# Decay attention with a squared-ReLU MLP: the weight loads issued from ScalarE's DMA queue

## The chip, the core and the metric

The kernel runs on one core of a Trainium2 chip. The core has five engines that run side by side, each with its own in-order stream of instructions: TensorE (PE in the profile; its weight loads are shown apart as PEld), VectorE (DVE), ScalarE (ACT), GpSimd (POOL) and SyncE (SP), which in this kernel does nothing but issue DMAs. They meet through semaphores. The metric is device time in microseconds; lower is better.

## The reference

Eight batches of eight heads, 576 positions, head size 64, so 64 heads (h counts them from 0) and 4608 tokens of width 512.

```python
scores = scale * q @ k.T                                # per head, 576 x 576
cum = cumsum(log(clip(f, 1e-4, 1)))
scores = where(causal, -1e9, scores + cum[:, None] - cum[None, :])
attn = exp(scores - max(scores)); attn /= attn.sum() + 1e-9
x = heads_side_by_side(attn @ v)                        # 4608 x 512
h = maximum(x @ w_in, 0)                                # w_in: 512 x 2048, float64
out = (h * h @ w_out).astype(float32)                   # w_out: 2048 x 512, float64
```

[...]

## The kernel before, in words

**Weights.** `weight_ops` is a generator that brings in 32 blocks of 128 rows by 512 doubles (512 KB each, `w0` to `w31`; even ones from `w_in`, odd ones from `w_out`) and turns each into a pair of 32-bit halves. Block by block it goes through: the load (line 172, `stage`), the magnitude on ScalarE (L181, `wmag`), a clamp and a shift on VectorE (L192, L197), two merges on VectorE (L202, L204, into `osb`), a rounding copy on ScalarE (L209) and a subtraction on GpSimd (L210). Two loads are issued at the start and then up to `DEPTH = 4` blocks ahead, at the point of the code that follows L204. Each block has a buffer of its own, so a load overwrites nothing that is in use.

**Attention.** A schedule written out by hand walks "slots", six to a head. For heads 0 to 13 one slot has a score matmul (L346, from the buffer `rl` that holds a head's q and k), a mask matmul (L348), an exponential on ScalarE (L362) and, two slots later, the product with v (L411, copied out by L425 and L426). The row maxima of the *next* head are found meanwhile: matmuls L313 from the buffer `rk`, a masked minimum on VectorE (L319, into `tcol`), and then five small DMAs per head (L325, `rl<-tcol`, 128 numbers each, 64 in the last) that lay the maxima as a row into that head's `rl`. They go from the last columns to the first: 448 to 575, 320 to 447, 192 to 319, 64 to 191, 0 to 63. The first score of a head takes columns 256 to 575, so it can start when the **first three** of its five rows have landed. Below, "the third row" is that third DMA.

**Around it.** Per head there is a load of `rk` (288 KB, L252, issued by GpSimd on a queue of its own), of `rl` (288 KB, L259), of v (160 KB, L266) and of two rows of decay (L246), and for every second head a normalisation: `cmp<-den` twice (L436), a reciprocal, `rdr<-cmp` (L441), `den<-rdr` twice (L444), then a product on GpSimd (L447). When the eight heads of a batch are done, VectorE splits the result (L464, L465) and the MLP starts (L477, L500), which from then on fills TensorE between the attention slots. From head 14 on another path with rounded halves is used; the weights are done by then.

**What sets the order.** At the end of the kernel `in_order` ties the instructions of TensorE, ScalarE, VectorE and GpSimd to the order in which the code wrote them. SP is not in that list: the order of its DMAs is the scheduler's, which works from its own estimate of when each can go. Every DMA that SP or ScalarE issues raises one of eight semaphores (DMAHW0 to DMAHW7), and before a semaphore is used again the issuing engine waits until the DMA that used it before has landed.

```python
LAG = 2                                   # slots from a score to its product with v
at((h - 1) * NU + int(x), int(2 * x) % 2, max_unit, h, i)   # maxima, a head ahead
in_order(tc, [getattr(mybir.EngineType, e) for e in ("PE", "Activation", "DVE", "Pool")])
```

Of the kernel before, what the change touches and what calls it, by code (L numbers as in the profile page):

```python
# [11 lines left out]
I32 = mybir.dt.int32  # L12
# [21 lines left out]
def decay_attention_relu2_kernel(  # L34
# [18 lines left out]
    nc = tc.nc  # L53
# [28 lines left out]
    def bank(use):  # L82
# [11 lines left out]
        out=mz[:, MW - P:], in_=mz[:, MW - P:], pattern=[[-1, P]],  # L94
# [6 lines left out]
        out=eye, in_=eye, pattern=[[-1, P]],  # L101
# [62 lines left out]
    def weight_ops():  # L164

        staged, mags = {}, {}

        def stage():
            i = len(staged)
            if i < NW:  # L170
                raw = staged[i] = wk.tile([P, 2 * DM], I32, name=f"w{i}", bufs=1)
                nc.sync.dma_start(out=raw, in_=(w_in, w_out)[i % 2][i // 2].bitcast(I32))

        def words(i):
            w = staged[i].rearrange("p (n t) -> p n t", t=2)
            return w[:, :, 0], w[:, :, 1]

        def magnitude(i):
            if i < NW:
                mags[i] = wk.tile([P, DM], F32, name="wmag", bufs=1)  # L180
                nc.scalar.activation(out=mags[i], in_=words(i)[1].bitcast(F32), func=AF.Abs)  # L181

        stage()
        stage()
        yield
        magnitude(0)
        yield
        for i in range(NW):
            low, high = words(i)
            mag = mags.pop(i)  # L190

            nc.vector.tensor_scalar(mag, mag, MAG_LOW, MAG_HIGH, ALU.max, ALU.min)  # L192
            yield
            w = wk.tile([P, DM], F32, name="osb")
            wi = w.bitcast(I32)

            nc.vector.tensor_scalar(  # L197
                wi, mag.bitcast(I32), 3, 0x3FFFFFFF, ALU.logical_shift_left, ALU.bitwise_and,
            )
            magnitude(i + 1)  # L200
            yield
            nc.vector.scalar_tensor_tensor(wi, high, -0x40000000, wi, ALU.bitwise_and, ALU.bitwise_or)  # L202
            yield
            nc.vector.scalar_tensor_tensor(wi, low, 29, wi, ALU.logical_shift_right, ALU.bitwise_or)  # L204
            while len(staged) < min(i + 1 + DEPTH, NW):
                stage()
            yield
            hl = wk.tile([P, 2, DM], F32R, name=f"w{i}", bufs=1)
            nc.scalar.copy(out=hl[:, 0], in_=w)  # L209
            nc.gpsimd.tensor_tensor(out=hl[:, 1], in0=w, in1=hl[:, 0].bitcast(F32), op=ALU.subtract)  # L210
            split_w.append(hl)
            yield
# [501 lines left out]
```

## Time and profile before

| | |
|---|---|
| device time, 3 runs | 1253.07 us median (1252.28 to 1254.52) |
| profiled execution | 1255.36 us, of which the span of the instructions is 1253.3 us |
| TensorE busy | 1193.5 us, 95% of the span |
| VectorE, ScalarE, GpSimd busy | 785.1, 702.0, 372.4 us |
| DMA | 71.90 MB, mean 57 GB/s |
| the 32 weight loads (L172) | issued between 1.4 and 165.5 us, all from SP |

A row of the timeline has the start, the duration, the engine, the line and what was done; in square brackets stands the engine's idle time just before it, and what ended that. Rows of SPq are the issuing of a DMA: how long the queue was occupied, not how long the data took. Rows with x2 or x3 give the stretch from the first to the end of the last. A row of `windows` has, for a stretch of the span, the busy time of each engine with its number of instructions in brackets, the granted clock, the share of time that the 16 DMA engines were busy, and GB/s.

### The profile page before, as it was taken

How to read it: one execution, taken by the hardware profiler on the slowest of the kernel's cores; microseconds unless marked ns; L12 is line 12 of the kernel's file. 1: busy time of each engine (PE TensorE's matmuls, PEld its weight loads, DVE VectorE, ACT ScalarE, POOL GpSimd, SP SyncE). 2: the span in 40 equal slices, each digit the busy share in tenths (PEclk: the TensorE clock that was granted, in tenths of full speed). 3: DMA queues.
4: the chain of work that ended last, by engine and by line, in shares of the span. 5: the costliest groups of instructions: out<-in, count | busy, mean ns of one | idle time of the engine just before them, and what ended most of it. 6: DMA issues, size and time to landing. Idle time of an engine off the chain costs nothing.

```text
span 1253.3 us, 23182 instructions
## 1 busy us (share of the span) xinstructions
PE 1193.5 (95%) x7652; PEld 1051.8 (84%) x7652; DVE 785.1 (63%) x2042; ACT 702.0 (56%) x1720; POOL 372.4 (30%) x512
## 2 busy tenths in 40 slices
PE   3877899999999999999999999999999999999998
PEld 2544687888989899999899989998998989999997
DVE  7658776666666767666656566667665766532332
ACT  3545455556666666665565556666666666632332
POOL 4323223333333333333322233334333333200000
PEclk9999999999999999999999999999999999999999
DMA  8857631112121112121201121211121212000000
GB/s 199 193 129 176 177 87 26 51 32 57 41 55 33 48 37 57 40 57 26 55 18 52 31 57 32 55 34 52 40 57 41 57 41 52 17 27 1 18 18 17
DMA packets 115639, 71.90 MB, mean 57 GB/s; under 512 B 97384, under 2 KB 97384, under 8 KB 115520
## 3 DMA queue, kind: packets, MB, share of 16 engines
q1 hardware_dynamic: 114400, 66.30, 21.7%
q0 software_dynamic: 1120, 4.13, 1.5%
q8 instruction: 61, 1.00, 0.3%
q14 instruction: 58, 0.48, 0.1%
HBM read 60.20 MB, written 9.88 MB: 56 GB/s over the span
## 4 chain that ended last, share of the span: by engine, by line
PE 63%; ACT 1%; issue 1%; POOL 1%; DMA 0%; DVE 0%; SPq 0%; POOLq 0%; DVEq 0%; ACTq 0%
PE bank L477 25%; PE bank L500 24%; PE bank L388 3%; PE bank L355 2%; PE bank L390 2%; PE bank L389 2%; PE bank L313 2%; PE bank L352 2%; DMA den<-rdr 0%; ACT ph L377 0%; ACT den L426 0%; ACT r L485 0%; ACT p L362 0%; POOL v L299 0%; ACT rl L281 0%
## 5 line engine op out<-in xcount | busy, mean ns | idle before, releaser
L500 PE MATMUL bank<-w,gh 128*128 128x512 f32 x1152 | 413.8, 400 | 0.0
L477 PE MATMUL bank<-xh,w 128*128 128x256 f32 x2304 | 330.7, 286 | 4.9 <-DVE tcol L319 4.9
L378 DVE TENSOR_TENSOR pl<-p,ph 128x320 fp32r<-128x320 f32 (+4 forms) x300 | 186.9, 623 | 206.6 <-ACT ph L377 197.1
L477 PEld LDWEIGHTS bank<-xh,w 128*128 128x128 f32 x2304 | 301.2, 190 | 13.8 <-DVE tcol L319 5.3
L500 PEld LDWEIGHTS bank<-w,gh 128*128 128x128 f32 x1152 | 217.6, 189 | 39.0
L485 ACT ACTIVATE r<-bank 128x256 f32<-128x256 f32 x288 | 110.4, 383 | 211.7 <-PE bank L477 198.3
L500 PE MATMUL bank<-w,gl 128*128 128x512 f32 x576 | 227.1, 394 | 0.2 <-DVE gl L488 0.2
L486 DVE TENSOR_TENSOR g<-r 128x256 f32<-128x256 f32 x288 | 127.3, 442 | 144.2 <-ACT r L485 143.4
L364 POOL TENSOR_SCALAR_AFFINE_SELECT p<-p 128x128 f32<-128x128 f32 (+1 forms) x250 | 81.5, 326 | 454.2 <-ACT p L362 313.5
L377 ACT CAST ph<-p 128x320 fp32r<-128x320 f32 (+4 forms) x300 | 124.4, 415 | 148.9 <-POOL p L364 147.1
L477 PE MATMUL bank<-xl,w 128*128 128x256 f32 x1152 | 185.3, 283 | 0.0
L319 DVE CUSTOM_DVE_ANT_0 bank<-bank,mz 128x256 f32<-128x256 f32 (+4 forms) x320 | 133.7, 432 | 45.9 <-PE bank L313 44.5
L477 PEld LDWEIGHTS bank<-xl,w 128*128 128x128 f32 x1152 | 158.9, 191 | 0.0
L362 ACT ACTIVATE p<-bank 128x320 f32<-128x320 f32 (+4 forms) x300 | 115.8, 386 | 71.7 <-PE bank L355 67.3
L488 DVE TENSOR_TENSOR gl<-g,gh 128x256 fp32r<-128x256 f32 x288 | 128.9, 448 | 35.7 <-ACT p L362 0.9
L313 PE MATMUL bank<-rk 66*128 66x320 f32 (+9 forms) x384 | 111.8, 318 | 24.8 <-DMA rk<-qkraw 13.4
L487 ACT ACTIVATE gh<-r 128x256 fp32r<-128x256 f32 x288 | 120.5, 418 | 9.1
L500 PEld LDWEIGHTS bank<-w,gl 128*128 128x128 f32 x576 | 109.3, 190 | 14.3 <-DVE gl L488 0.9
L313 PEld LDWEIGHTS bank<-rk 66*128 66x128 f32 (+3 forms) x384 | 68.7, 185 | 40.1 <-DVE tcol L319 17.1
L388 PE MATMUL bank<-pl,vh 128*65 128x320 f32 (+4 forms) x350 | 99.4, 284 | 1.6 <-ACT den L426 1.4
L389 PE MATMUL bank<-ph,v 128*64 128x320 f32 (+4 forms) x350 | 94.8, 271 | 0.0
L390 PE MATMUL bank<-ph,vh 128*65 128x320 f32 (+4 forms) x350 | 93.0, 271 | 0.0
(71 smaller groups left out, 1498.2 us busy)
## 6 DMA issues: line engine op xcount, KB each, us to landing
qkraw<-in_qk SPq DMA_DIRECT2D x50, 288.0 KB
v<-in_v SPq DMA_DIRECT2D x64, 160.0 KB
den<-rdr SPq DMA_DIRECT2D x64, 144.0 KB
out<-osb SPq DMA_DIRECT2D x36, 256.0 KB
w<-in_w_in SPq DMA_DIRECT2D x16, 512.0 KB
w<-in_w_out SPq DMA_DIRECT2D x16, 512.0 KB
rl<-in_qk SPq DMA_DIRECT2D x14, 288.0 KB
rk<-in_qk POOLq DMA_DIRECT2D x14, 288.0 KB, 4.7
```

What stands on the lines that cost most here:

```text
L313: nc.tensor.matmul(ps[:m, :n], st["r2"][:rows, q0:q0 + m], st["kl0"][:rows, k0:k0 + n], start=True, stop=True,)
L319: nc.vector.tensor_tensor_reduce(out=ps[:m, :n], in0=ps[:m, :n], in1=mz[:m, mo:mo + n], op0=ALU.add, op1=ALU.min, scale=-1.0, scalar=init, ...
L377: nc.scalar.copy(out=ph[:kn, :n], in_=p[:kn, :n])
L378: nc.vector.tensor_tensor(out=pl[:kn, :n], in0=p[:kn, :n], in1=ph[:kn, :n].bitcast(F32), op=ALU.subtract,)
L388: nc.tensor.matmul(acc[:D + 1, o], vh, pl[:kn, i], start=first, stop=False)
L389: nc.tensor.matmul(acc[:D, o], vl, ph[:kn, i], start=False, stop=False)
L390: nc.tensor.matmul(acc[:D + 1, o], vh, ph[:kn, i], start=False, stop=last)
L477: nc.tensor.matmul(ph[:, :T], w[:, s, cc], x[:, cc, :], start=(cc == 0 and k == 0), stop=(cc == NCC - 1 and k == 2),)
L486: nc.vector.tensor_tensor(out=g, in0=r, in1=r, op=ALU.mult)
L487: nc.scalar.activation(out=gh, in_=r, func=AF.Square)
L488: nc.vector.tensor_tensor(out=gl, in0=g, in1=gh.bitcast(F32), op=ALU.subtract)
L500: nc.tensor.matmul(po, g[:, ts], w[:, s], start=(fc == 0 and k == 0), stop=(fc == NF - 1 and k == 2),)
```

## The change

The one call that issues a weight load is made on ScalarE in place of SP. ScalarE's stream gets 32 DMA instructions, SP's loses them.

```diff
         def stage():
             i = len(staged)
             if i < NW:
                 raw = staged[i] = wk.tile([P, 2 * DM], I32, name=f"w{i}", bufs=1)
-                nc.sync.dma_start(out=raw, in_=(w_in, w_out)[i % 2][i // 2].bitcast(I32))
+                nc.scalar.dma_start(out=raw, in_=(w_in, w_out)[i % 2][i // 2].bitcast(I32))
```

ScalarE is in the list of `in_order`, so a load now stands where the code wrote it. The streams of TensorE, VectorE and GpSimd are the same as before; ScalarE's computing instructions keep their order; SP's is rearranged in its first 150 DMAs.

**SP at the start.** Numbers such as 138 tell buffers apart: `w_100`, `w_102`, `w_136`, `w_138`, `w_140`, `w_168` are blocks 0 to 5. SP before, from the decay's store to the last maxima of head 0:

```order
L152 DMA cum_dr<-qkraw 64x576
L259 DMA rl<-in_qk 64x1152
L246 DMA rk_77<-cum_dr 2x576
L246 DMA rl<-cum_dr 2x576
L172 DMA w_138<-in_w_out 128x1024
L172 DMA w_140<-in_w_in 128x1024
L325 DMA rl<-tcol 1x128x1 x3
L172 DMA w_168<-in_w_out 128x1024
L325 DMA rl<-tcol 1x128x1
L266 DMA v<-in_v 128x5x64
L325 DMA rl<-tcol 1x64x1
```

SP now, at the same place:

```order
L259 DMA rl<-in_qk 64x1152
L246 DMA rl<-cum_dr 2x576
L237 DMA qkraw<-in_qk 64x1152
L325 DMA rl<-tcol 1x128x1 x3
L246 DMA rk_76<-cum_dr 2x576
L325 DMA rl<-tcol 1x128x1
L325 DMA rl<-tcol 1x64x1
```

The weight loads are gone from around the three rows that head 0's first score needs; a load of `qkraw` (288 KB, for head 14) that stood far later is now ahead of them, and three loads of v, which are not in this piece, have moved to the very start.

**ScalarE at the start.** ScalarE now, with the semaphores that each instruction waits for (the engine's name for a computing engine, DMAHW for a landed DMA):

```order
L181 ACTIVATE wmag<-w_100 128x512 [waits DMAHW0_49]
L181 ACTIVATE wmag<-w_102 128x512 [waits DMAHW3_49,DVE_49]
L172 DMA w_136<-in_w_in 128x1024 [waits DMAHW2_49]
L172 DMA w_138<-in_w_out 128x1024 [waits DMAHW5_49]
L172 DMA w_140<-in_w_in 128x1024 [waits DMAHW7_49]
L209 CAST w_142<-osb 128x512 [waits DVE_49,Activation_49]
L181 ACTIVATE wmag<-w_136 128x512 [waits DMAHW2_49,DVE_49]
L172 DMA w_168<-in_w_out 128x1024 [waits DMAHW5_49]
L209 CAST w_174<-osb 128x512 [waits DVE_49,Activation_49]
```

Blocks 2, 3 and 4 stand behind the second magnitude, which waits for VectorE, and each waits for a DMA that has to land first.

**ScalarE and SP between heads 5 and 6.** `w_628` and `w_682` are blocks 13 and 14. ScalarE now; before, the rows are the same without the two DMAs:

```order
L362 ACTIVATE ph_612<-bank3_609 128x192
L172 DMA w13_628<-in_w_out 128x1024
L362 ACTIVATE pl_633<-bank1_630 64x64
L209 CAST w9_638<-osb_600 128x512
L362 ACTIVATE ph_644<-bank2_641 128x448
L362 ACTIVATE pl_655<-bank3_652 128x256
L181 ACTIVATE wmag_660<-w11_485 128x512
L362 ACTIVATE ph_666<-bank1_664 128x320
L425 COPY xt0_289<-bank0_614 64x320
L426 COPY den_669<-bank0_614 1x320
L172 DMA w14_682<-in_w_in 128x1024
L362 ACTIVATE pl_687<-bank2_684 128x320
```

SP before, from the end of head 5's maxima to those of head 6:

```order
L325 DMA rl<-tcol 1x64x1
L172 DMA w_628<-in_w_out 128x1024
L246 DMA rk_77<-cum_dr 2x576
L441 DMA rdr<-cmp 128x9
L259 DMA rl<-in_qk 64x1152
L246 DMA rl<-cum_dr 2x576
L325 DMA rl<-tcol 1x128x1
L172 DMA w_682<-in_w_in 128x1024
L444 DMA den<-rdr 64x576 x2
L325 DMA rl<-tcol 1x128x1 x3
```

SP now has the same rows there without the two weight loads. Head 3 is where more than that differs. SP before:

```order
L325 DMA rl<-tcol 1x128x1
L436 DMA cmp<-den 64x1x9 x2
L325 DMA rl<-tcol 1x128x1 x3
L172 DMA w_428<-in_w_in 128x1024
L266 DMA v<-in_v 128x5x64
L325 DMA rl<-tcol 1x64x1
```

SP now, at head 3:

```order
L325 DMA rl<-tcol 1x128x1
L436 DMA cmp<-den 64x1x9
L325 DMA rl<-tcol 1x128x1
L266 DMA v<-in_v 128x5x64
L436 DMA cmp<-den 64x1x9
L325 DMA rl<-tcol 1x128x1 x2
L325 DMA rl<-tcol 1x64x1
```

A load of v has moved ahead of head 3's third row; block 10 (`w_428`), which was issued behind that row, is now issued by ScalarE.

## The prediction

> **What bounds the kernel now.** After the busy line of the page (TensorE at 95%) I read the windows that cut the span where its character changes, then TensorE's timeline in the stretch with idle time.
>
> ```profile
> 0.00:13.40 13.40, 0.00 (x0) 0.00 (x0) 9.36 (x12) 5.29 (x7) 7.67 (x21) 1.00 0.80 206
> 13.40:134.20 120.80, 86.79 (x375) 58.41 (x376) 83.56 (x224) 60.14 (x138) 38.13 (x46) 0.97 0.75 176
> 134.20:200.00 65.80, 64.25 (x369) 53.52 (x370) 48.35 (x109) 33.59 (x80) 17.60 (x17) 0.98 0.35 97
> 200.00:1253.30 1053.30, 1042.44 (x6910) 939.83 (x6908) 643.88 (x1698) 603.03 (x1497) 309.00 (x430) 1.00 0.16 39
> ```
>
> TensorE sets the time. After 134.2 us it is busy for 64.25 of 65.80 and 1042.44 of 1053.30 us: nothing that happens to loads there can move the end much. Its idle time is in front: 13.40 us before the first matmul and 120.80 - 86.79 = 34.0 us up to the MLP's first matmul. All but seven of the 32 loads fall before that point (the 25th is the row at 130.09 further down), so what the change is worth is decided there, and a microsecond won there is one at the end. Where TensorE waits:
>
> ```profile
> 23.00 0.87 PE L346 MATMUL bank<-rl 128*128 128x320 f32 x1 [5.30 <-DMA w<-in_w_out]
> 50.13 0.51 PE L346 MATMUL bank<-rl 128*128 128x320 f32 x1 [2.19 <-DMA rl<-tcol]
> 60.17 0.54 PE L346 MATMUL bank<-rl 128*128 128x320 f32 x1 [2.37 <-DMA rl<-tcol]
> 69.91 0.51 PE L346 MATMUL bank<-rl 128*128 128x320 f32 x1 [1.77 <-issue]
> 82.59 0.76 PE L346 MATMUL bank<-rl 128*128 128x320 f32 x1 [4.68 <-DMA rl<-tcol]
> 93.45 0.51 PE L346 MATMUL bank<-rl 128*128 128x320 f32 x1 [1.56 <-DMA rl<-tcol]
> 104.33 0.51 PE L346 MATMUL bank<-rl 128*128 128x320 f32 x1 [2.63 <-DMA rl<-cum_dr]
> ...
> 126.70 1.75 POOL L447 TENSOR_TENSOR xt<-xt,den 128x576 f32<-128x576 f32 x1 [0.74 <-DMA den<-rdr]
> 128.49 1.75 DVE L464 CAST xh<-xt 128x1024 fp32r<-128x1024 f32 x1 [1.29 <-POOL xt L447]
> 134.20 2.08 PE L477 MATMUL bank<-xh,w 128*128 128x256 f32 x8 [4.93 <-DVE tcol L319]
> ```
>
> The seven L346 rows are the first scores of heads 0, 3, 4, 5, 6, 7 and 8. Their waits sum to 20.5 us. The releaser's name varies, but I take all seven for the third row of maxima: that is the DMA issued last among what the score reads. The eighth wait, 4.93 us, is the MLP's start; VectorE was late there because `den` landed late, 1.29 us of its time.
>
> **Why the third row is late.** A small DMA that nothing stands before, and one with bulk around it:
>
> ```profile
> 43.08 2.13 SPq L436 DMA_DIRECT2D cmp<-den  x2
> 45.17 0.85 POOL L252 DMA_DIRECT2D rk<-in_qk  x1 [3.96 <-PE bank L313]
> 46.40 1.17 SPq L325 DMA_DIRECT2D rl<-tcol  x2
> 46.54 0.96 DVE L438 TENSOR_SCALAR cmp<-cmp 128x9 f32<-128x9 f32 x1 [0.63 <-DMA cmp<-den]
> 47.62 0.60 SPq L172 DMA_DIRECT2D w<-in_w_in  x1
> ```
>
> The `cmp` pair is issued by 45.21 and VectorE goes on at 46.54: 1.33 us after the end of the issue. Head 3's third row is the first of the two at 46.40, issued by about 46.98, yet its score starts at 50.13: 3.15 us, with no weight load near, but with GpSimd's 288 KB on another queue, issued at 45.17. So two things hold the third row: loads in flight on *any* queue, and loads ahead on SP's own. The rows where weights stand ahead:
>
> ```profile
> 15.98 0.36 SPq L172 DMA_DIRECT2D w<-in_w_out  x1
> 16.39 0.43 SPq L172 DMA_DIRECT2D w<-in_w_in  x1
> 16.92 1.81 SPq L325 DMA_DIRECT2D rl<-tcol  x3
> ...
> 68.35 0.59 SPq L172 DMA_DIRECT2D w<-in_w_out  x1
> 69.36 0.34 SPq L441 DMA_DIRECT2D rdr<-cmp  x1
> 73.52 0.59 SPq L172 DMA_DIRECT2D w<-in_w_in  x1
> 74.20 2.09 SPq L444 DMA_DIRECT2D den<-rdr  x2
> 76.38 2.11 SPq L325 DMA_DIRECT2D rl<-tcol  x3
> 98.67 0.58 SPq L172 DMA_DIRECT2D w<-in_w_out  x1
> 99.30 1.15 SPq L325 DMA_DIRECT2D rl<-tcol  x2
> ```
>
> Head 0: two loads ahead, third row issued by 18.73, score at 23.00, 4.27 us. Less the quiet 1.33 that is 2.9 us for two loads, 1.5 us each, my price of a load that is in the way.
>
> **When the loads go now.** A load stands behind a ScalarE instruction; the ends of these in the trace of before tell when it can go:
>
> ```profile
> 10.72 0.67 ACT L181 ACTIVATE wmag<-w 128x512 f32<-128x512 f32 x1 [1.42 <-DVE osb L197]
> 65.02 0.33 ACT L362 ACTIVATE ph<-bank 128x192 f32<-128x192 f32 x1
> 71.70 0.42 ACT L426 COPY den<-bank 1x320 f32<-1x320 f32 x1
> 96.74 0.36 ACT L426 COPY den<-bank 1x256 f32<-1x256 f32 x1
> ```
>
> Blocks 3 and 4 go from 11.4 us instead of 15.98, block 13 at 65.4 instead of 68.35, block 14 at 72.1 instead of 73.52, block 17 at 97.1 instead of 98.67. So the loads come 1.4 to 4.6 us sooner (block 2, formerly among the first, later). Those that stood ahead of a third row clear earlier; those that stood behind one move into its window, beside GpSimd's load.
>
> **The terms**, gains as plus, ends in brackets.
> - Head 0: +2.0 (0 to 2.9). Two loads leave SP's queue and are early, but `qkraw`'s 288 KB is new there, and by the order the third row waits on the semaphore that block 4 raises; so not the whole price.
> - Head 3: -1.5 (-0.6 to -2.1). A load of v now stands ahead of its third row, at least an issue (0.60, as at 47.62), at most that and one load's 1.5. Block 10 comes earlier too. I take the upper half.
> - Heads 5 and 7: -1.0 and -0.5 (0 to -1.5 each). Block 13, and by the same order block 16, moves from behind the last row to the time of the third; one load's price is the end.
> - Head 6: +1.5 (0 to 4.7, its whole wait). Block 13 no longer precedes `rdr`, nor block 14 `den`, for which SP waits with the three rows behind it; one load's price.
> - Head 8: +2.0 (0.6 to 2.6). Block 17 was between its rows: 0.58 us of issue, and one load's 1.5; its wait is the cap.
> - Head 4: 0; no load of weights between its rows before or now. Its wait stays, by GpSimd's load.
> - MLP's start: +1.0 (0 to 1.3). The chain that ends in `den` passes block 20 here:
>
> ```profile
> 115.65 0.35 SPq L172 DMA_DIRECT2D w<-in_w_in  x1
> 116.09 1.07 SPq L441 DMA_DIRECT2D rdr<-cmp  x1
> 122.52 1.13 SPq L444 DMA_DIRECT2D den<-rdr  x2
> 130.09 0.34 SPq L172 DMA_DIRECT2D w<-in_w_in  x1
> ...
> L172 SPq DMA_DIRECT2D w<-in_w_out x16: 343/500/627, 2.1 to 165.5; - x16
> ...
> PEld bank L411 <- ACT pl L362: 2.2, 4, 1.0
> ...
> DVE xt L138 <- DMA xt<-in_f: 0.6, 1, 0.6
> ```
>
> `rdr` to `den` took 6.4 us there. The gain cannot pass VectorE's 1.29 us of waiting; after that its own work is next.
> - ScalarE: -0.5 (0 to -11.2). On SP an issue took 0.34 to 0.63 us; I take the same, 0.45, on ScalarE, for the trace has none there. 25 loads before 134.2 us make 11.2 us. ScalarE is busy 60.14 of 120.80 us, and TensorE's largest wait for it at the products with v is 2.2 us in all. In seven heads a late exponential only shortens the wait for the third row, which does not depend on ScalarE. That cover is why the term is small; without it each load costs its 0.45. The seven loads after 134.2 lie beside 64.25 us of TensorE work: 0, or 3.2 if that cover went.
> - The start: -0.3 (0 to -1.5). `in_f`, which was alone, now goes beside block 0; VectorE already waits 0.6 us for it, and a load's price is the end. The v loads at the head of SP's queue go while it has nothing else to issue: 0.
>
> The sum is 2.0 - 1.5 - 1.5 + 1.5 + 2.0 + 1.0 - 0.5 - 0.3 = +2.7 us. The profiled execution took 1255.36 us, of which the span is 1253.3; that would become 1252.7. The median of the runs, 1253.07, lies 2.3 us under that execution, and less 2.7 it is **1250.4 us**.
>
> **The rivals.**
> - *The gates stay.* Being on another queue and somewhat earlier does nothing; only SP's time for issuing is saved: 0.36 + 0.43, 0.59 + 0.59 and 0.58, 2.6 us ahead of third rows, against 0.6, 1.5, 0.5 and 0.3 of losses above. That is -0.3: 1253.4. For it speaks head 3, held with a load on another queue alone; against it, that the loads' times do shift. [...]
> - *ScalarE becomes the gate* (slower). Its stream is in order, so a load that waits for its semaphore, or whose issue is long, stops the exponential behind it, then the product with v two slots later. Fully exposed it is 11.2 us against gains of 3.2: 1261; half exposed, 1255.5. I put it at 1258. It decides from about 0.2 us a load on TensorE's path ((2.7 + 2.5) / 25). Against it: the cover above, and that by the order loads mostly wait for DMAs that were issued long before.
> - *The gates open.* Heads 0, 6, 8 and the MLP's start gain their upper ends, 11.5 us, and heads 5 and 7 lose nothing: less 0.6, 0.5 and 0.3 it is 10.1, so 1243.0. Against it: VectorE finishes the maxima not much earlier than SP issues them, and GpSimd's load stays.
>
> That the change does not do what it says is excluded by the order.
>
> **How the numbers follow.** A measurement of this kernel tells about 0.2%, 2.5 us, from no change. Forecast, 0.36, of which 0.29 is over that bound and 0.07 within; the gates stay, 0.27, within; ScalarE, 0.22, slower; the gates open, 0.15, faster. Faster 0.44, same 0.34, slower 0.22. The forecast's own range is 1247 to 1252.5. The range of 8 in 10 reaches down to the open gates and up to most of ScalarE's case: 1243 to 1257.
>
> **What would show it.** The waits before L346 at heads 0, 6 and 8 shrink, those at heads 3 and 5 grow, that of head 4 stays; L464 waits less for L447; ScalarE's idle time before L362 shrinks by about 0.45 us a load while the product's wait for it hardly grows. I am wrong if the sum of the seven waits stays near 20 us, if waits of L411 for L362 reach 5 us, or if anything after 200 us changes by over 1 us.

## The result: slower by 0.6%, and the profile after

The changed kernel took **1262.77 us** (median of 7 runs, 1259.53 to 1264.3) against 1254.52 us for the kernel before (7 runs, 1251.19 to 1259.52) beside it: a ratio of **1.0057, 95% interval 1.0033 to 1.0081**. Timed once more later, 1261.65 against 1254.93 us, 1.0056 (1.0037 to 1.0076). The ratios with intervals, here and below, are estimated from the runs of both kernels; they are not quotients of two medians, which would be 1.0066 here. The prediction, 1250.4 us and faster, was wrong, and its range ended at 1257.

The profiled execution of the changed kernel took 1259.53 us, the quickest of the seven, with a span of 1257.8 us. First the windows, cut at this kernel's own first matmul (17.51 us) and its MLP's start (140.11 us); columns as before.

```profile
0.00:17.51 17.51, 0.00 (x1) 0.03 (x1) 7.23 (x12) 4.67 (x6) 7.17 (x20) 1.00 0.93 220
17.51:140.11 122.60, 87.11 (x375) 58.72 (x375) 85.08 (x224) 60.65 (x139) 39.13 (x46) 0.95 0.71 167
140.11:206.00 65.89, 65.03 (x368) 53.88 (x369) 48.36 (x109) 33.55 (x80) 17.15 (x17) 0.96 0.34 92
206.00:1257.80 1051.80, 1040.70 (x6911) 938.71 (x6909) 641.85 (x1698) 603.10 (x1497) 307.23 (x430) 1.00 0.16 39
```

From the MLP's start on it took 65.89 + 1051.80 = 1117.7 us, against 1119.1 before; in all profiles here it is between 1115.8 and 1119.1. So, as the prediction held, the loss is decided in front. What it missed is the first row: the first matmul is 4.1 us later, 17.51 against 13.40. The stretch from there to the MLP took 122.60 instead of 120.80.

A profile is a single execution, and this stretch varies from one to the next. A second profile of the same kernel, of a run of 1263.01 us, has this row for it:

```profile
17.32:144.59 127.27, 91.37 (x376) 61.75 (x376) 87.40 (x224) 60.90 (x139) 39.05 (x46) 0.91 0.67 161
```

The MLP's start is 4.5 us later there, and nearly all of that is TensorE's busy time, 91.37 instead of 87.11 us, at a lower granted clock, 0.91 instead of 0.95. So a wait or a start read from one profile says where time goes, and only the medians say which kernel is slower. TensorE's waits in the first profile, from its timeline:

```profile
17.51 0.82 PE L313 MATMUL bank<-rk 128*128 128x256 f32 x2 [17.51 <-DMA rk<-qkraw]
29.37 1.41 PE L346 MATMUL bank<-rl 128*128 128x320 f32 x2 [6.74 <-DMA rl<-tcol]
46.80 0.78 PE L346 MATMUL bank<-rl 128*128 128x320 f32 x2 [1.83 <-issue]
58.07 0.78 PE L346 MATMUL bank<-rl 128*128 128x320 f32 x2 [3.06 <-DMA rl<-tcol]
67.67 0.78 PE L346 MATMUL bank<-rl 128*128 128x320 f32 x2 [1.94 <-issue]
78.09 0.78 PE L346 MATMUL bank<-rl 128*128 128x320 f32 x2 [2.48 <-DMA rl<-tcol]
88.62 0.78 PE L346 MATMUL bank<-rl 128*128 128x320 f32 x2 [2.53 <-DMA rl<-tcol]
99.72 0.81 PE L346 MATMUL bank<-rl 128*128 128x320 f32 x2 [3.46 <-DMA rl<-tcol]
110.05 0.78 PE L346 MATMUL bank<-rl 128*128 128x320 f32 x2 [0.46 <-DMA rl<-tcol]
...
140.11 2.07 PE L477 MATMUL bank<-xh,w 128*128 128x256 f32 x8 [3.92 <-DVE tcol L319]
```

The rows are heads 0, 2, 3, 4, 5, 6, 7 and 8. Head 2, at 46.80, did not wait before. Against the starts shown before, head 3 is late by 7.9 us (58.07 - 50.13), head 6 by 6.0, head 8 by 5.7 and the MLP by 5.9. So all of the loss arises by head 3, and heads 6 and 8 give back 2 us of it. SP's timeline, at the start and at heads 2 and 3:

```profile
1.46 0.57 SPq L259 DMA_DIRECT2D rl<-in_qk  x1
2.08 2.52 SPq L266 DMA_DIRECT2D v<-in_v  x3
9.87 1.33 SPq L244 DMA_DIRECT2D rk<-qkraw  x2
...
20.26 0.51 SPq L237 DMA_DIRECT2D qkraw<-in_qk  x1
20.82 1.94 SPq L325 DMA_DIRECT2D rl<-tcol  x3
...
40.08 0.48 SPq L325 DMA_DIRECT2D rl<-tcol  x1
40.67 0.62 SPq L266 DMA_DIRECT2D v<-in_v  x1
41.38 3.22 SPq L325 DMA_DIRECT2D rl<-tcol  x4
...
50.77 0.55 SPq L325 DMA_DIRECT2D rl<-tcol  x1
51.42 0.61 SPq L266 DMA_DIRECT2D v<-in_v  x1
52.13 0.59 SPq L436 DMA_DIRECT2D cmp<-den  x1
52.84 2.17 SPq L325 DMA_DIRECT2D rl<-tcol  x3
```

`rk<-qkraw` (the first matmul's last input) was issued at 9.87 and let it go at 17.51. Three loads of v stand ahead of it. Head 0's third row, third of the group at 20.82, has the load of `qkraw` ahead. At heads 2 and 3 a load of v (for heads 3 and 4) has slipped in ahead of the third row. None of these is a weight load: they are SP's other DMAs, which the scheduler put in a new order once the weight loads had left. Counted from the start they are the fourth and the fifth load of v. Before the change the fourth stood between the fourth and the fifth row of head 3, and the fifth in the same place at head 4: the first five loads of v have all moved ahead.

### The profile page after: what moved, and what is told of

The parts are those of the page before. It is cut to its first block, busy times and chain, and to the rows that moved or that the text cites. A ratio compares the mean times of both kernels' runs of the same rounds, so it can differ in the third digit from the quotient of the medians.

```text
span 1257.8 us, 23157 instructions
## 1 busy us (share of the span) xinstructions
PE 1192.8 (95%) x7652; PEld 1051.3 (84%) x7652; DVE 782.5 (62%) x2042; ACT 702.0 (56%) x1720; POOL 370.7 (29%) x512
## 4 chain that ended last, share of the span: by engine, by line
PE 76%; ACT 3%; issue 1%; DVE 1%; POOL 1%; DMA 1%; SPq 0%; DVEq 0%; POOLq 0%; ACTq 0%
PE bank L477 30%; PE bank L500 28%; PE bank L388 4%; PE bank L313 3%; PE bank L355 3%; PE bank L390 3%; PE bank L389 3%; PE bank L352 3%; DMA den<-rdr 0%; ACT r L485 0%; ACT p L362 0%; ACT den L426 0%; ACT ph L377 0%; ACT gh L487 0%; ACT rl L281 0%
```

## The experiments

The median of the kernel before was 1255.31 us in the first group of four runs, 1254.65 in the second, 1255.12 in the third and 1254.93 in the fourth; each ratio is against the kernel before on the same chip. Most kernels below fix SP's order: a function ties SP's first 158 DMAs (190 where weights are on SP) one behind another, as `in_order` does for the other engines. Only the list differs. The tie by itself, on the scheduler's own new order, was not run.

```diff
-    in_order(tc, [getattr(mybir.EngineType, e) for e in ("PE", "Activation", "DVE", "Pool")])
+    sp_in_order(tc, SP_ORDER); in_order(tc, [getattr(mybir.EngineType, e) for e in ("PE", "Activation", "DVE", "Pool")])
```

**1. The order or the queue.** The changed kernel, with SP's DMAs in the order of before, less the weight loads:

```diff
 weight loads: nc.scalar.dma_start      # as changed
-SP_ORDER: the scheduler's
+SP_ORDER: as before the change, without L172
```

> The changed kernel with SP's DMAs tied to the order that they had before the change (the 32 weight loads stay on ScalarE). Theory O (the rearranged order on SP is what costs): the first matmul starts at 13.4 to 15 us instead of 17.5, head 0's first score before 25 us, the MLP's first matmul at or before 134 us, and the ratio to before is 0.996 to 1.001. Theory Q (the second queue is what costs: weight loads from ScalarE run beside SP's small DMAs at the start, whatever SP's order): first matmul still at 16.5 us or later and a ratio of 1.004 to 1.008.

Measured: 1255.29 us, ratio **0.9992 (0.9977 to 1.0008)**. The queue by itself is worth nothing that shows, by the interval between -2.9 and +1.0 us; the rearranged order carries the loss. TensorE's waits in this kernel:

```profile
12.61 0.82 PE L313 MATMUL bank<-rk 128*128 128x256 f32 x2 [12.61 <-DMA rk<-qkraw]
24.59 1.41 PE L346 MATMUL bank<-rl 128*128 128x320 f32 x2 [6.71 <-DMA rl<-tcol]
52.50 0.78 PE L346 MATMUL bank<-rl 128*128 128x320 f32 x2 [2.25 <-issue]
62.21 0.81 PE L346 MATMUL bank<-rl 128*128 128x320 f32 x2 [2.04 <-DMA rl<-tcol]
72.52 0.78 PE L346 MATMUL bank<-rl 128*128 128x320 f32 x2 [2.35 <-DMA rl<-tcol]
82.61 0.78 PE L346 MATMUL bank<-rl 128*128 128x320 f32 x2 [2.08 <-issue]
93.80 0.78 PE L346 MATMUL bank<-rl 128*128 128x320 f32 x2 [3.56 <-DMA v<-in_v]
103.64 0.78 PE L346 MATMUL bank<-rl 128*128 128x320 f32 x2 [0.20 <-issue]
...
134.55 2.08 PE L477 MATMUL bank<-xh,w 128*128 128x256 f32 x8 [6.01 <-DVE tcol L319]
```

Heads 6 and 8 wait 2.08 and 0.20 instead of 4.68 and 2.63, 5.0 us less, as the prediction said in kind. Against that, head 0 waits 1.4 more, head 7 2.0 more and the MLP's start 1.1 more; head 2 does not wait. The MLP starts 0.35 us later than before. The gains are there and are given back.

Head 0's longer wait begins on SP, at the copy of the decay (L246) that stands ahead of the rows:

```profile
13.14 0.60 SPq L259 DMA_DIRECT2D rl<-in_qk  x1
18.57 0.32 SPq L246 DMA_DIRECT2D rk<-cum_dr  x1
19.33 2.46 SPq L325 DMA_DIRECT2D rl<-tcol  x4
```

SP waited 4.8 us there for the decay's store (`cum_dr<-qkraw`, issued at 10.49 and 12.50) to land; before the change it waited 1.2 us, and the rows went from 16.92 and not from 19.33. ScalarE issues blocks 2 to 4 between 10.73 and 12.33 us in this kernel, while before blocks 3 and 4 went at 15.98 and 16.39, behind that wait. From 10 to 20 us the DMA engines moved 266 GB/s here and 183 before. So the weight loads now run beside the store; that they are what makes it late fits these numbers and was not tested by itself. The wait is 4.5 to 5.5 us in the five profiles with the weights on ScalarE and the old order at the start.

**2. The two loads moved at the start, one at a time,** each in the kernel of experiment 1:

```diff
 L259 rl<-in_qk
+L266 v<-in_v  x3        # a_v_early, and b_v_early with the weights on SP
 L244 rk<-qkraw x2
 ...
 L246 rl<-cum_dr
+L237 qkraw<-in_qk       # a_q_early
 L325 rl<-tcol x3
```

> As the kernel with SP's old order, but the three loads of v that the change moved to the very start (heads 0, 1, 2) stand there again; everything else on SP as before. Theory O, with the v loads as the cause of the late first matmul: first matmul at 16.5 to 17.5 us, and 3 to 4 us more time than with the old order. Theory Q: no different from the old order within 1 us.

> As the kernel with SP's old order, but the load of qkraw for head 14 stands ahead of head 0's rows of maxima, as the change has it. Theory O, with qkraw as the cause of head 0's longer wait: first matmul as with the old order, the wait before head 0's first score 1 to 3 us longer than with the old order, and that much more time. Theory Q, or block 5 as the cause of that wait: no difference over 0.5 us at head 0.

> The kernel before (all weight loads on SP) with only the three v loads moved to the start, behind the load of rl, as the change has them. Theory O: first matmul 2 to 4 us later than 13.4, ratio 1.002 to 1.004, without any load on ScalarE. Theory Q: 13.4 to 14, ratio 1.000.

Measured: with the v loads early 1255.52 us, 1.0002 (0.9989 to 1.0014); with `qkraw` early 1255.76 us, 1.0006 (0.9990 to 1.0021); in the kernel before, the v loads early cost 1256.74 us, 1.0020 (1.0003 to 1.0037). With the v loads early the first matmul started at 17.29 and not at 12.61, but head 0's wait fell from 6.71 to 4.21 us, and the MLP started 0.8 us later. With `qkraw` early head 0 waited 7.97 us, and the MLP again started 0.8 us later. Theory O had the late first matmul right, and on ScalarE's queue its cost wrong: 3 to 4 us were expected of the v loads. Neither alone is the loss.

**3. The start and the rest, halved.** `c_start` has the new order up to head 0's first row and the old one behind; `c_mid` the old start and the new order behind it, with the load of v for head 2 ahead of head 2's rows; `c_vq` makes both moves of experiment 2.

> The changed kernel with SP's order as after the change only up to the first row of head 0 (three v loads and the load of head 14's q and k moved to the start, the two reads and copies of the start rearranged), and the order of before from there on. Theory S (the loss is the start: the v loads delay the first matmul, head 14's load delays head 0's third row, and the two add up): first matmul near 17.5, head 0's scores near 29, MLP's start near 139 to 140, 1260 to 1263 us. Theory M (the loss is the rearranged places at heads 2 and 3, where the loads of v for heads 3 and 4 go ahead of third rows): MLP's start near 136, 1255.5 to 1257.5 us.

> The changed kernel with SP's order of before up to head 0's rows and as after the change behind them: the loads of v for heads 3 and 4 ahead of the third rows of heads 2 and 3, one row copy ahead of the last rows of heads 0 and 1, one of the two small copies of head 1's sums later (and the v load of head 2 four places earlier, ahead of its rows). Theory S: as the version with all of the old order, head 0's scores near 24.6, MLP's start near 134.6, 1255 to 1256.5 us. Theory M: head 0's scores near 24.6 but the waits of heads 2 and 3 grow by 2 to 3 us, MLP's start 137 to 139, 1258 to 1262 us.

> The old SP order in the changed kernel, with four moves only: the three v loads to the start and head 14's load ahead of head 0's rows. Theory S, in the form that these two loads together do it: first matmul near 17.3, head 0's scores near 28.5 to 29.5 (26.6 with the v loads alone, plus the 1.7 that head 14's load cost alone), MLP's start 138 to 140, 1259 to 1262 us. If it is the rearranged reads and copies of the start (one read of sums ahead of two reads of the rows): head 0's scores near 27, 1256 to 1257 us, with the version of the whole start at 1260 or more. Theory M: 1256 to 1257 us.

| kernel | median and ratio | first matmul | head 0's score | head 2's wait | MLP's start |
|---|---|---|---|---|---|
| order of before (1) | 1255.29, 0.9992 | 12.61 | 24.59 | none | 134.55 |
| c_vq | 1257.67, 1.0028 (1.0013 to 1.0043) | 15.65 | 27.47 | none | 136.95 |
| c_start | 1258.46, 1.0031 (1.0018 to 1.0044) | 17.29 | 28.87 | none | 138.68 |
| c_mid | 1260.39, 1.0045 (1.0025 to 1.0064) | 12.88 | 24.58 | 2.60 | 137.80 |
| changed | 1262.77, 1.0057 (1.0033 to 1.0081) | 17.51 | 29.37 | 1.83 | 140.11 |

The last four columns are single profiles and do not rank the kernels. Theories S and M were each half right: both halves cost, the start 3.9 us by its ratio, the rest 5.6 us (with the load of v for head 2 in a place that neither kernel has). At the start, `c_vq` is most of `c_start`. Against experiment 1's ratio the v loads cost 0.0010 alone, `qkraw` 0.0014 and both together 0.0036; with intervals of about 0.0015 either way that does not tell a plain sum from more than a sum.

**4. The loads of v for heads 3 and 4.** In the changed kernel they alone are put back, to the rows of heads 3 and 4 (`m_v_back`; its text below says heads 2 and 3, but the order that was run has them a head later). In the kernel of experiment 1 and in the kernel before, they are moved ahead (`n_v34`, `b_v34`). There the load for head 2 has to go ahead of head 2's rows too; in the changed kernel it stands at the start. The last text is for the changed kernel timed again beside those two.

```diff
 L325 rl<-tcol            # head 2, first row
+L266 v<-in_v             # for head 3
 L325 rl<-tcol x4
 ...
 L325 rl<-tcol            # head 3, second row
+L266 v<-in_v             # for head 4
 L325 rl<-tcol x2
-L266 v<-in_v             # for head 3
 L325 rl<-tcol
 ...
 L325 rl<-tcol            # head 4, fourth row
-L266 v<-in_v             # for head 4
 L325 rl<-tcol
```

> The changed kernel with SP's order as after the change, except that the loads of v for heads 3 and 4 go back to their old places, between the fourth and the fifth row of heads 2 and 3. If these two loads are what the places at heads 2 and 3 cost: no wait at head 2, MLP's start near 138.5, 1257.5 to 1259.5 us, as with the whole new start and the old rest. If the copy of sums and the row copies moved there are the cost: head 2 or 3 still waits 2.5 us or more, MLP's start near 140, 1261 to 1263 us.

> The changed kernel with SP's old order, except that the loads of v for heads 3 and 4 stand where the change put them, behind the first row of head 2 and behind the second row of head 3 (and the load of v for head 2 ahead of head 2's rows, which their order of buffers asks for). If these two loads are the larger part of the loss: a wait near 2.5 us at head 2, 0.5 to 1 us more at head 3, MLP's start 136.5 to 138.5, 1258 to 1260.5 us. If they cost only beside the new start: MLP's start near 135, 1255 to 1256.5 us.

> The kernel before (weights on SP) with the same two loads of v moved ahead (and that of head 2 with them). If the place of these loads on SP costs whatever queue the weights are on: a wait of 2 us or more at head 2, 1257.5 to 1261 us. If it costs only where the weights do not stand in line with them: within 1.5 us of before.

> The changed kernel as it is, timed beside its parts. By its first comparison a ratio of 1.0033 to 1.0081: 1259 to 1265 us. If the parts add up (1.0016 to 1.0031 for the start, 1.002 to 1.0045 for the rest), 1259 to 1264.5 us.

Measured: put back, 1257.60 us, 1.0016 (1.0000 to 1.0032), no wait of note at head 2 and the MLP at 138.26. Moved alone, 1260.40 us, **1.0052 (1.0035 to 1.0070)**, beside 1.0056 for the whole change. In the kernel before, with the weights on SP, 1258.81 us, 1.0030 (1.0014 to 1.0046). The cleanest of the three is the first: two loads of 160 KB, each about a head too early in SP's queue, cost 0.0040, 5.0 us. The other two, 6.5 us with the weights on ScalarE and 3.8 us with the weights on SP, contain the move of head 2's load as well. Whether the parts add is open: 1.0052 with `m_v_back`'s 1.0016 lies within the whole change's interval, with `c_start`'s 1.0031 above it, and each part has an interval of its own. TensorE's rows of `n_v34`, heads 0, 2, 3, 5 and 7:

```profile
25.68 1.40 PE L346 MATMUL bank<-rl 128*128 128x320 f32 x2 [7.65 <-DMA rl<-tcol]
45.10 1.44 PE L346 MATMUL bank<-rl 128*128 128x320 f32 x2 [2.88 <-DMA rl<-tcol]
58.27 1.03 PE L346 MATMUL bank<-rl 128*128 128x320 f32 x2 [3.33 <-DMA rl<-tcol]
78.34 0.78 PE L346 MATMUL bank<-rl 128*128 128x320 f32 x2 [2.88 <-DMA v<-in_v]
100.38 1.40 PE L346 MATMUL bank<-rl 128*128 128x320 f32 x2 [4.54 <-DMA rl<-tcol]
```

Head 2's wait is new, 2.88 us, and head 3's is 1.1 us longer than in experiment 1; heads 4, 6 and 8 do not wait. Behind the two waits the matmul pair is longer, 1.44 and 1.03 us instead of 0.78. The windows show the granted clock there, first of `n_v34` behind the waits of heads 2 and 3, then of experiment 1's kernel from head 2's first score:

```profile
45.00:48.40 3.40, 3.30 (x7) 2.33 (x8) 0.49 (x2) 1.18 (x3) 0.00 (x0) 0.50 0.37 95
58.70:62.10 3.40, 3.40 (x10) 2.24 (x9) 1.48 (x5) 1.27 (x3) 0.00 (x0) 0.50 0.42 113
```

```profile
41.10:44.50 3.40, 3.40 (x19) 2.75 (x18) 1.61 (x6) 2.00 (x6) 1.31 (x2) 1.00 0.95 262
```

The granted clock was 0.50 for the 3.4 us behind both waits: TensorE looks full and does 7 and 10 matmuls, where in experiment 1's kernel it did 19 behind head 2's first score and 16 behind head 3's, at 1.00. The same follows head 2's wait of 2.48 us in `b_v34`, of 2.60 in `c_mid` (the pair took 1.44 us in both) and of 2.28 in the changed kernel's second profile, and head 6's wait of 4.68 us in the kernel before (0.52). It does not follow head 2's 1.83 us or head 3's 3.06 us in the changed kernel's first profile (1.00 behind both). A long pair alone does not tell it: head 0's took 1.41 us there at a granted clock of 1.00. From the first matmul to the MLP's start, `n_v34` and then experiment 1's kernel:

```profile
12.77:142.52 129.75, 92.96 (x375) 62.39 (x375) 89.16 (x224) 60.36 (x139) 38.83 (x46) 0.91 0.68 167
12.61:134.55 121.94, 85.49 (x375) 57.83 (x375) 85.61 (x224) 60.82 (x139) 39.02 (x46) 0.98 0.71 178
```

Of the 8.0 us between the two starts of the MLP, 7.5 are TensorE's busy time; its idle time is 36.8 and 36.5 us. So in this pair of profiles the new wait was made up for at other heads, and the clock, 0.91 against 0.98 granted, makes the difference. The pair overstates it: the mean granted clock of all runs is 0.990 for `n_v34` and 0.992 for experiment 1's kernel, whose profile had 0.996. As an estimate, that difference, 0.0022 before rounding, of 1255 us is at most 2.8 us of the 5.1 us between the two medians. The loss of the whole change against the kernel before cannot be put down to the clock: its mean over all runs is 0.991 for both.

**5. Weight blocks 0 to 2 later on SP, in the kernel before.**

```diff
-L172 w<-in_w_in, w<-in_w_out
 L259 rl<-in_qk
-L172 w<-in_w_in
 L244 rk<-qkraw x2
 ...
 L152 cum_dr<-qkraw
+L172 w<-in_w_in, w<-in_w_out, w<-in_w_in
```

> The kernel before (weights on SP), with the first three weight loads moved behind the reads of head 0's q and k: they no longer go to the queue while in_f and the first rows are loading. If the DMA engines, nearly full over the first 13 us, set the first matmul: it starts 1 to 2 us earlier than 13.4, head 0's scores near 21.5 to 22.5, and 1253 to 1255 us, since some of the start's gain is lost again at the waits of heads 3 to 8. If only the chain of scan, reads and copies sets it: first matmul near 13.4, no change; if the three loads then collide with the copies of head 0: first matmul near 14.5 and slower by 1 us.

Measured: 1260.56 us, 1.0038 (1.0022 to 1.0054). The first matmul came at 12.71, 0.7 us sooner, and then this happened, on VectorE:

```profile
17.84 0.43 DVE L192 TENSOR_SCALAR wmag<-wmag 128x512 f32<-128x512 f32 x1 [7.95 <-ACT wmag L181]
```

VectorE waited 7.95 us for block 0, which its order puts ahead of head 0's maxima; head 0's score came at 26.48 instead of 23.00. None of the three expectations had that. So a load that was issued later held up an engine whose order has the load's consumer in front, by 7.95 us here, with everything behind it.

**6. Holding back GpSimd's loads.** In the kernel before, the 288 KB of `rk` for the head after next run over the third row of heads 3, 4, 5 and 7, each for 1.6 to 1.8 us. The edit waits for the head's first exponentials first:

```diff
-                at((h - 3) * NU + 3, 0, load_rounded, h)
+                at((h - 2) * NU, 0, behind_score, h - 2); at((h - 2) * NU, 0, load_rounded, h)
+        def behind_score(h):
+            g = wk.tile([P, 1], F32, name="late"); nc.gpsimd.tensor_copy(out=g[:1, :], in_=state[h]["p"][0][:1, :1])
```

> The kernel before (weights on SP, its order on SP kept), with the loads of q and k into rk on POOL's queue, heads 2 to 13, held back until the head two before has its first exponentials: a small copy on POOL that reads them stands ahead of each load. In before, these 288 KB loads run from 46.7 to 48.5, 56.9 to 58.6, 66.7 to 68.2 and 90.4 to 92.0 us, each over the third row of heads 3, 4, 5, 7, which lands 4 us after its issue instead of 2. Theory G (this load makes the seven waits): the third rows land about 2 us after issue, the sum of the seven waits falls from 20.5 to 6 to 12 us, MLP's start 124 to 128, 1241 to 1248 us. Rival (the third row waits for the weight and v loads or for VectorE's chain whatever POOL does): the sum stays at 17 to 21, 1253 to 1256 us. Rival of the other sign: the load comes too late for the maxima two heads on, new waits before the first matmul of a head, 1258 us or more.

> The same hold on POOL's loads, in the changed kernel with SP's old order (weights on ScalarE's queue). Theory G: MLP's start 124 to 128, 1241 to 1248 us, within 2 us of the version with the weights on SP if the queue of the weights does not matter there either. Rival: 1253 to 1256 us.

Measured: with the weights on SP 1257.89 us, 1.0021 (1.0003 to 1.0039); on ScalarE, with the old order on SP, 1254.17 us, 0.9989 (0.9971 to 1.0006), the lowest median here but not told apart from before. Theory G fails: the MLP starts at 141.18 and 138.02 us in the two profiles, where it had 124 to 128. TensorE's rows with the weights on SP, and one of GpSimd's:

```profile
39.50 0.78 PE L346 MATMUL bank<-rl 128*128 128x320 f32 x2 [1.72 <-DMA rl<-tcol]
62.20 1.44 PE L346 MATMUL bank<-rl 128*128 128x320 f32 x2 [5.17 <-DMA rl<-tcol]
85.82 1.41 PE L346 MATMUL bank<-rl 128*128 128x320 f32 x2 [5.12 <-DMA rl<-tcol]
108.45 1.38 PE L346 MATMUL bank<-rl 128*128 128x320 f32 x2 [4.07 <-DMA rl<-tcol]
```

```profile
51.19 0.56 POOL L252 DMA_DIRECT2D rk<-in_qk  x1 [0.32 <-PE bank L313]
```

Heads 3, 5 and 7 no longer wait, which fits that GpSimd's load held their third row. But heads 4, 6 and 8 (62.20, 85.82, 108.45) now wait 5.17, 5.12 and 4.07 us. With no wait at head 3 the load goes at 51.19, next to SP's own 288 KB of `rl` at 51.13 and a weight load at 52.17; head 4's third row, issued by 55.9, lets its score go only at 62.20. Which of these loads holds it is not separated. With head 0's 4.07 the waits of heads 0 to 8 still sum to 20.2 us, and yet the MLP starts 7.0 us later than before: 6.7 us of that is TensorE's busy time, 93.48 instead of 86.79 us. Behind each of the three long waits the granted clock was 0.50 or 0.51 for 3.4 us, and its mean over the 12 runs is 0.988, against 0.991 before. In this profile fewer and longer waits of the same sum cost more than many short ones. No version tried here is faster than the kernel before by more than its interval.

## Why the prediction was wrong, point by point

Of the gains it named some came; the losses that it set at nothing, or left out, were larger. Waits and starts of the first profile after, against before (single profiles both):

| term | predicted | measured |
|---|---|---|
| the start | -0.3 | **-4.1** (first matmul 13.43 to 17.51) |
| head 0 | +2.0 | **-1.4** (5.30 to 6.74) |
| head 2 | no term | **-1.8** (0 to 1.83) |
| head 3 | -1.5 | -0.9 (2.19 to 3.06) |
| head 4 | 0 | +0.4 (2.37 to 1.94) |
| heads 5 and 7 | -1.5 | -2.6 (1.77 to 2.48, 1.56 to 3.46) |
| head 6 | +1.5 | +2.2 (4.68 to 2.53) |
| head 8 | +2.0 | +2.2 (2.63 to 0.46) |
| MLP's start | +1.0 | +1.0 (4.93 to 3.92) |
| ScalarE | -0.5 | 0 (waits for exponentials 2.2 in both) |

The measured column sums to -5.0; the MLP's start moved by -5.9. Of the remaining 0.9, 0.3 us is TensorE's busy time (87.11 against 86.79 us); the rest lies in shorter waits that are not broken down here.

- **The failed step is the one that read SP's new order.** "The v loads at the head of SP's queue go while it has nothing else to issue: 0" priced the time of issuing and not what the loads occupy afterwards. Issuing took 2.52 us; `rk<-qkraw`, issued within 0.8 us of its old time, then let TensorE go at 17.51 instead of 13.43. With the v loads alone moved it went at 17.29, with the old order at 12.61. So the v loads delay it, and neither the queue nor `in_f` beside block 0 does, although VectorE's wait for `in_f` grew from 0.6 to 3.5 us. How much of this reaches the end is another matter: the v loads alone left the time at 1.0002, the whole new start made it 1.0031.
- **Head 2 was left out.** The prediction read head 3's piece as one load of v that slips ahead by two rows. It is head 4's load; head 3's own had left for the rows of head 2, which the prediction did not look at. Experiment 4 gives 5.0 us for the two, where the prediction had 1.5 for one of them. One row of that reading was taken wrongly too: before the change head 3 did not wait "with no weight load near", since block 10 is issued at 47.62 and the score starts at 50.13.
- **Head 0's gain was not there even with the old order** (6.71 us against 5.30). The term counted the two loads that left SP's queue and not the decay's store and copies ahead of the rows, at which SP then waited 4.8 us instead of 1.2 (experiment 1). In the changed kernel SP waited 3.9 us there, and blocks 3 and 4 went at 13.77 and 17.10 us, not from 11.4.
- **Heads 3, 5, 6, 8 and the MLP's start** were right in sign, and head 4 near nothing. Head 7's loss was undersized, 1.9 us instead of 0.5. In the second profile of the changed kernel these heads have the same signs (2.65, 3.07, 0.26 and 1.22 us), but the wait before the MLP's start is 6.00 us, so that gain is not shown.
- **ScalarE** was rightly small. Its issues, here two of ScalarE's rows after, take 0.33 and 0.34 us, and TensorE's wait for exponentials at the products with v is the same 2.2 us in all (row of the waits after: total, times, longest):

```profile
13.77 0.33 ACTq L172 DMA_DIRECT2D w<-in_w_out  x1
50.55 0.34 ACTq L172 DMA_DIRECT2D w<-in_w_in  x1
```

```profile
PEld bank L411 <- ACT pl L362: 2.2, 4, 1.0
```

- **The rivals.** "The gates stay" is nearest to what the queue alone does, in the time and not wait by wait: with the old order 0.9992, and the sum of the seven waits was 20.5 before, 20.7 and 17.2 in the two profiles after, and 19.2 in experiment 1. The prediction named that sum as the sign of being wrong. It leaves out head 2's new wait, 1.83 and 2.28 us. Of its other two signs, the waits of L411 stayed at 2.2 us, and the stretch from 65.9 us behind the MLP's start took 1.5 us less, which is within the spread of the profiles. "ScalarE becomes the gate", the only slower case, had the right sign and the wrong mechanism; no rival was "the scheduler's new order costs", though the order was in hand.
- **The time of "the gates stay".** No run shows by itself that only SP's time for issuing is saved; what was measured is the whole, 0.9992 (0.9977 to 1.0008) in experiment 1. The rival's 1253.4 us is 1.0003 of the 1253.07 before and lies in that interval; the kernel as changed differs by the order.

Not settled: why the waits of heads 0 to 8 sum to much the same whatever is moved, 17.8 to 22.5 us in fifteen of the sixteen profiles (14.6 in `a_v_early`). Experiment 6 shows waits changing heads, not the reason for the sum. Nor is it shown what part of the differences between the kernels with a fixed order the half clock makes, or how the loads of v hold up a read that is issued 5 us behind them.

## What to carry to other kernels

When an edit takes instructions out of a queue that a scheduler orders, the new place of everything that stays is part of the change: price each such move as if it had been made by hand, for what it holds after it is issued, and look at every consumer, not the one that was noticed. Where a small DMA gates the busiest engine, the place of a bulk load ahead of it can matter more than the choice of queue: here 5.0 us for two loads of v, and nothing that shows for 32 weight loads on the other queue. To separate the two, keep the edit and fix the old order: that single kernel told queue from order here. And before the cost of a move is read from a wait in two profiles, look at the busy time and the clock of the stretch around it.

## What the runs showed of the hardware

- A wait of TensorE can cost more than itself: behind head 2's waits of 2.28 to 2.88 us the granted clock was 0.50 or 0.51 for one stretch of 3.4 us in four profiles (`n_v34`, `b_v34`, `c_mid` and the changed kernel's second). Behind waits of 2.19, 2.37 and 2.63 us (the kernel before, heads 3, 4 and 8) and of 2.48, 2.53 and 3.06 us (the changed kernel's first profile, heads 5, 6 and 3) it was 1.00. So the length of a wait did not decide it by itself; what did is not shown.
- Issuing a weight load took 0.33 to 0.36 us on ScalarE for 30 of the 32 loads (0.38 and 0.45 us for the first two), against 0.34 to 0.63 us on SP (the changed kernel and the kernel before).
